# A linear-attention and MLP block on one core: one tile's transpose moved to TensorE, the first block's reciprocals moved to DMA, and the written orders laid out anew

## The chip, the cores and the metric

The kernel runs on one core of a Trainium2 chip. The metric is the device time of one execution in microseconds; the times below are medians of several runs. A profile of one execution goes with them, with every instruction's start and length on each engine: TensorE (PE, its weight loads as PEld), VectorE (DVE), ScalarE (ACT), GpSimd (POOL), and the DMA queue that SyncE (SP) issues.

## The reference

x has 2048 rows of 512 values in bf16. The kernel computes a linear attention with 32 heads of 16 columns and then a two-layer ReLU network of inner width 1792, each on normalized rows and each added to what came in.

```python
qkv = layernorm(x) @ wqkv                     # q, k, v: 32 heads of 16
phi = lambda t: where(t > 0, t + 1, exp(t)) + 1e-6
pq, pk = phi(q), phi(k)
kv  = einsum("bhsd,bhse->bhde", pk, v)
z   = einsum("bhsd->bhd", pk)
num = einsum("bhqd,bhde->bhqe", pq, kv)
den = einsum("bhqd,bhd->bhq", pq, z)[..., None] + 1e-6
h   = x + (num / den) @ wo
h2  = h + relu(layernorm(h) @ w1) @ w2
```

## The kernel before

The 2048 rows lie in 16 tiles of 128 rows (index t) and in four chunks, called blocks here too, of four tiles (index c). The whole program is one list of words, `ORDER`, written out by hand or by a planner; each word is the name of an `op_` function with its indices, and each engine executes its own instructions strictly in the order in which the words stand. Semaphores between the engines are put in from the data that the words read and write. So a word that waits holds up every later word on its engine. All DMAs are issued by SP, in the order of their words.

The words that matter here, with the engine that executes them:

- `lx.t.n` (SP, line 201) loads n tiles of x from tile t on; `lk`, `lq`, `lv`, `lo`, `l1`, `l2` load parts of the weights (line 204).
- `S.t`, `A.t` (VectorE, lines 222 and 223) take mean and variance of tile t; `R.t.n` (ScalarE, lines 228 and 229) the reciprocal deviation by a logarithm and an exponential; `N.t` (VectorE, line 247) writes the normalized tile. Lower-case `s`, `a`, `r`, `n` do the same after the attention.
- A normalized tile has to be transposed into `lnT`, 128 columns by 128 rows four times. Either TensorE does it (`T.t.b`, line 266, into PSUM bank b) and ScalarE copies it out (`E.t`, line 276), or one DMA does it (`X.t`, line 287; `x.t` after the attention, line 288). Before, tiles 0 to 3 go by TensorE and the others by DMA.
- `K.t.b` and `Q.c.j.b` (TensorE, lines 295 and 303) are the projections, four matmuls of 512 columns each. phi takes `F` (exponential, ScalarE, line 313), `U` (ReLU, ScalarE, line 316), `M` (minimum, VectorE, line 320) and `D` (sum, VectorE, line 323); `W` (VectorE, line 328) does the work of U and D in one instruction that reads PSUM. With a q in front (`qF` ...) they work on Q.
- `G.t` (TensorE, line 347) sums the normalized rows times phi(K) over the tiles, in PSUM banks 4 to 7; `za`, `zf`, `z`, `zc`, `zh` sum phi(K) alone. `gD` (VectorE) or `gA` (ScalarE) copies G out, `kv` multiplies it by the weights of v, `kx` masks the heads, `m` multiplies by wo and `mA` copies that out.
- The denominators: `dn.c` (TensorE, line 444) for the four tiles of a chunk, `dnl` (ScalarE, line 450) the logarithm, `dnx.c.t.n` (ScalarE, line 457) the exponential of its negative for n tiles, spread over the columns. The reciprocals are then transposed into `rd`: by a DMA (`dt.t`, line 476), or by TensorE and ScalarE (`rt.t.b`, line 266, and `re.t`, line 468). `dm.c.j.2` (VectorE, line 480) multiplies phi(Q) by them, and `h.t.b` (TensorE, line 490) multiplies by m; `hD` (VectorE, line 496) adds x.
- The network: `p.c.f.b` (TensorE, line 506), `pA` or `pD` (ReLU by ScalarE, line 512, or VectorE, line 517), `f` (TensorE, line 526), `fo` (VectorE, line 534), `fd` (SP, line 541) writes out.

TensorE starts with `warm` matmuls on zeros while the first tiles come in. The tile buffer `rd` holds the reciprocals of one chunk, so each chunk's `dt` waits for the `dm` of the chunk before.

Of the kernel before, what the change touches and what calls it, by code (L numbers as in the profile page):

```python
# [38 lines left out]
p.0.11.1 p.0.8.2 p.0.10.0 dt.14 dt.13 dt.15 f.3.7.0.7 pA.0.10.2 pA.0.8.2 n.5 dt.12 n.6 dm.3.0.2 dm.3.2.2 n.4
s.11 n.7 hD.8 h.14.1 h.13.3 f.0.4.7.7 h.12.0 h.15.6 hD.14 s.10 s.8 s.14 hD.12 s.9 x.5 x.7 x.6 x.4 f.1.5.7.7  # L40
f.3.7.7.7 fo.0 hD.15 p.1.9.1 p.1.8.0 f.2.6.0.7 pA.1.8.2 f.2.6.7.7 p.1.0.0 p.1.1.1 fo.1 a.14 a.10 a.8 fo.3 s.12
a.11 a.12 s.15 a.15 n.11 hD.13 s.13 a.13 a.9 n.8 n.10 p.1.3.3 n.9 n.12 pA.1.0.2 fo.2 x.10 fd.3 x.9 x.8 x.11
p.1.10.6 p.1.4.0 p.1.7.5 fd.0 p.1.5.1 p.1.2.2 p.1.11.7 p.1.6.4 n.14 pD.1.6.2 r.12.4 pA.1.4.2 n.15 n.13
pD.1.10.2 pA.1.2.2 p.2.4.0 p.2.5.1 pA.2.4.2 x.15 f.5.5.0.7 p.2.0.0 p.2.1.1 p.2.2.2 p.2.3.3 pA.2.0.2 p.1.13.1
f.7.7.0.7 p.1.12.0 f.4.4.0.7 pD.2.2.2 pD.1.12.2 p.2.7.3 p.2.6.2 p.2.13.1 f.6.6.0.7 f.7.7.7.7 f.5.5.7.7
p.2.12.0 r.4.4 pD.2.6.2 p.2.10.2 f.6.6.7.7 pA.2.12.2 x.12 x.14 x.13 fd.1 fd.2 p.2.9.1 p.2.11.3 p.2.8.0 fo.7
pA.2.10.2 pD.2.8.2 f.4.4.7.7 p.3.3.3 p.3.9.1 p.3.8.0 fo.4 pA.3.8.2 fo.5 fo.6 f.8.4.0.7 p.3.5.1 p.3.4.0 p.3.2.2
f.9.5.0.7 pD.3.4.2 pD.3.2.2 fd.5 fd.4 p.3.0.0 f.10.6.0.7 f.9.5.7.7 f.10.6.7.7 p.3.6.2 p.3.7.3 p.3.1.1 fd.6
f.8.4.7.7 pD.3.6.2 pA.3.0.2 r.8.4 fo.9 fo.10 p.3.13.1 f.11.7.0.7 p.3.11.3 p.3.12.0 pA.3.12.2 fo.8 f.11.7.7.7
fd.7 fd.9 p.3.10.2 f.12.4.0.7 f.14.6.0.7 fo.11 pD.3.10.2 f.15.5.0.14.3.1 f.12.4.7.7 f.14.6.7.7 fd.8 fd.10  # L50
fd.11 fo.15.3.1 fo.12 fo.14 f.13.5.0.7 f.13.5.7.7 fo.13 f.15.7.0.14.0.2 fd.12 fd.14 fd.13 fd.15.3.1
f.15.4.0.14.2.1 fo.15.0.2 fd.15.0.2 fo.15.2.1 fd.15.2.1
"""


# [521 lines left out]
```

## Time and profile before

| what | value |
|---|---|
| median of 3 runs | 169.99 us (169.94 to 171.55) |
| profiled execution: own time, span | 171.34 us, 169.6 us |
| TensorE busy (share of the span) | 162.6 us (96%) |
| VectorE, ScalarE, GpSimd busy | 102.6, 65.2, 4.9 us |
| granted TensorE clock | 1.00 |
| DMA transposes into lnT before and after the attention, and into rd | 12, 16 and 15 |

The span runs from the first to the last instruction of the profiled execution; its own time, as the runs are timed, is 1.74 us more. Busy times are sums of an engine's records; matmuls are pipelined, so that a record of a 512-column matmul (380 ns on average) is longer than the distance between the starts of two of them (0.216 us). Times of start are microseconds from the span's start. A bracket behind a line of the timeline gives the engine's idle time ahead of it and what ended it.

### The profile page before, as it was taken

The numbers are of one execution on the slowest core, as the hardware profiler recorded it, in microseconds if no ns is written. First come the engines' busy times: TensorE is split into PE (matmuls) and PEld (weight loads), VectorE is DVE, ScalarE is ACT, GpSimd is POOL, SyncE is SP. The second block draws the span as 40 slices with busy tenths as digits, with TensorE's granted clock in tenths as the row PEclk, the third lists the DMA queues.
The fourth block names the chain that finished last, engine by engine and source line by source line (L and its number), as shares of the span: only waits on it lengthen the run. The fifth ranks groups of instructions, "written<-read, shape, count | busy, mean of one in ns | idle before, by whom it ended". The sixth has DMA issues, their size and how long they took to land.

```text
span 169.6 us, 2272 instructions
## 1 busy us (share of the span) xinstructions
PE 162.6 (96%) x847; PEld 75.6 (45%) x863; DVE 102.6 (61%) x203; ACT 65.2 (38%) x98; POOL 4.9 (3%) x21
## 2 busy tenths in 40 slices
...
GB/s 128 312 192 142 110 81 125 270 395 261 65 122 203 108 64 66 62 31 95 60 69 0 9 115 62 69 120 1 0 0 0 124 0 4 0 93 31 0 66 62
DMA packets 31675, 15.75 MB, mean 93 GB/s; under 512 B 24240, under 2 KB 30640, under 8 KB 31664
## 3 DMA queue, kind: packets, MB, share of 16 engines
...
q8 instruction: 7, 0.11, 0.3%
...
HBM read 7.86 MB, written 2.10 MB: 59 GB/s over the span
## 4 chain that ended last, share of the span: by engine, by line
PE 83%; DMA 7%; DVE 5%; SPq 2%; issue 2%; ACT 0%; DVEq 0%
PE bk L526 28%; PE bk L506 28%; PE bk L490 9%; PE bk L303 6%; PE bk L347 6%; PE bk L295 4%; DMA x_nat<-in_A_x_dram 3%; DMA lnT<-h_nat 2%; DVE st L222 2%; DMA rd<-wk_sb 2%; SPq L201 1%; DVE h_nat L247 1%; DVE eb L320 1%; PE bk L444 1%; PE bk L388 1%
## 5 line engine op out<-in xcount | busy, mean ns | idle before, releaser
L526 PE MATMUL bk<-w_sb,at 128*128 128x512 bf16 (+2 forms) x248 | 51.2, 355 | 0.2
L506 PE MATMUL bk<-lnT,w_sb 128*128 128x512 bf16 x220 | 50.9, 380 | 0.2
L512 ACT ACTIVATE at<-bk 128x1024 bf16<-128x1024 f32 x17 | 17.2, 1022 | 67.3 <-PE bk L506 60.9
L526 PEld LDWEIGHTS <-at 128*128 128x128 bf16 x252 | 23.5, 98 | 25.2
L506 PEld LDWEIGHTS <-w_sb 128*128 128x128 bf16 x224 | 21.7, 98 | 26.0
L517 DVE TENSOR_SCALAR at<-bk 128x1024 bf16<-128x1024 f32 x11 | 13.4, 1223 | 32.7 <-PE bk L506 32.6
L534 DVE SCALAR_TENSOR_TENSOR gT<-bk,rstd,h_nat 128x512 bf16<-128x512 f32 (+2 forms) x18 | 12.0, 688 | 15.9 <-PE bk L526 14.8
L313 ACT ACTIVATE eb<-bk 128x1024 bf16<-128x1024 f32 (+1 forms) x18 | 16.4, 924 | 4.0 <-PE bk L295 2.4
L295 PE MATMUL bk<-wk_sb,lnT 128*128 128x512 bf16 x63 | 15.3, 380 | 0.7 <-DMA lnT<-h_nat 0.5
L490 PE MATMUL bk<-m_sb,pqs 128*128 128x512 bf16 x61 | 15.1, 380 | 0.2
L303 PE MATMUL bk<-lnT,wq_sb 128*128 128x512 bf16 x61 | 14.6, 379 | 0.1
L496 DVE TENSOR_TENSOR h_nat<-bk,x_nat 128x512 bf16<-128x512 f32 x16 | 10.8, 684 | 4.7 <-PE bk L490 4.7
L316 ACT ACTIVATE rb<-bk 128x1024 bf16<-128x1024 f32 (+1 forms) x14 | 12.5, 901 | 2.6 <-PE bk L303 1.9
L347 PE MATMUL bk<-at,h_nat 128*128 128x512 bf16 x56 | 13.4, 379 | 0.1
L222 DVE BATCH_NORM_STATS2 st<-x_nat 128x6 f32<-128x512 bf16 x16 | 10.7, 677 | 3.1 <-DMA x_nat<-in_A_x_dram 3.1
L224 DVE BATCH_NORM_STATS2 st<-h_nat 128x6 f32<-128x512 bf16 x16 | 10.7, 682 | 0.1
L347 PEld LDWEIGHTS <-h_nat 128*128 128x128 bf16 x64 | 6.2, 98 | 8.7 <-issue 1.5
L490 PEld LDWEIGHTS <-pqs 128*128 128x128 bf16 x64 | 5.9, 98 | 8.7 <-DVE pqs L480 2.0
L295 PEld LDWEIGHTS <-lnT 128*128 128x128 bf16 x64 | 6.0, 98 | 8.3 <-DMA lnT<-h_nat 1.4
L303 PEld LDWEIGHTS <-wq_sb 128*128 128x128 bf16 x64 | 6.1, 97 | 6.9
L457 ACT ACTIVATE wk_sb<-ld 128x1024 bf16<-128x1024 f32 (+1 forms) x9 | 8.2, 951 | 0.1
L480 DVE TENSOR_TENSOR pqs<-pqT,rd 128x1024 bf16<-128x1024 bf16 x8 | 5.2, 685 | 4.4 <-DMA rd<-wk_sb 2.6
...
## 6 DMA issues: line engine op xcount, KB each, us to landing
...
```

What stands on the lines that cost most here:

```text
L222: op_S = lambda t: nc.vector.bn_stats(out=st[:, t, :], in_=x_nat[:, t, :])
L295: nc.tensor.matmul(bk[:, b, :], lhsT=lnT[c][:, kd, j * P : (j + 1) * P], rhs=wk_sb[:, kd, :], start=(kd == 0), stop=(kd == KD - 1),)
L303: nc.tensor.matmul(bk[:, b, :], lhsT=wq_sb[:, kd, j * P : (j + 1) * P], rhs=lnT[c][:, kd, :], start=(kd == 0), stop=(kd == KD - 1),)
L313: nc.scalar.activation(out=buf(eb, kind, i, n), in_=bank(at_bank[kind, i], n), func=ACT.Exp)
L316: nc.scalar.activation(out=buf(rb, kind, i, n), in_=bank(at_bank[kind, i], n), func=ACT.Relu)
L347: nc.tensor.matmul(bk[:, KD + kd, :], lhsT=ln_nat[:, t, kd * P : (kd + 1) * P], rhs=pk(t)[:, 0, :], start=(t == 0), stop=(t == NT - 1),)
L490: nc.tensor.matmul(bk[:, b, :], lhsT=pqs[:, (c * KD + jb) % NQ, j * P : (j + 1) * P], rhs=m_sb[:, jb, :], start=(jb == 0), stop=(jb == KD ...
L506: nc.tensor.matmul(bk[:, b, cols], lhsT=w1_sb[:, kd, f * P : (f + 1) * P], rhs=lnT[c][:, kd, cols], start=(kd == 0), stop=(kd == KD - 1),)
L512: nc.scalar.activation(out=acts[c % 2][:, f : f + n, :], in_=bank(at_bank["p", c, f], n), func=ACT.Relu)
L517: nc.vector.tensor_scalar(out=acts[c % 2][:, f : f + n, :], in0=bank(at_bank["p", c, f], n), scalar1=0.0, scalar2=None, op0=ALU.max,)
L526: nc.tensor.matmul(bk[:, b, 0 : w * P], lhsT=acts[c % 2][:, f, j * P : (j + 1) * P], rhs=w2_sb[:, f, k * P : (k + w) * P], start=(f == 0), ...
L534: nc.vector.scalar_tensor_tensor(out=o_t[:, t % NO, cols], in0=bk[:, at_bank["f", t, k], 0 : w * P], scalar=rstd2[:, t : t + 1], in1=h_nat ...
```

## The change

Nothing is computed in another way, and no function that runs is altered (`op_warmq` is added and not called). The list `ORDER` is written anew:

- `X.5` (a DMA) is replaced by `T.5.0` and `E.5` (TensorE and ScalarE). The transposes T.2, T.1 and T.3 go to banks 0, 7 and 6, K.0 and K.1 to banks 4 and 7.
- `rt.3.3` and `re.3` (TensorE and ScalarE) are replaced by `dt.3` (a DMA), and the two exponentials `dnx.0.3.1` and `dnx.0.2.1` by one, `dnx.0.2.2`.
- `W` on VectorE and `U` with `D` are exchanged in four places: `W.14`, `qW.0.2` and `qW.3.2` become U and D, `qU.1.0` with `qD.1.0` becomes `qW.1.0`. `gD.2.2` becomes `gA.2.2` (ScalarE). The ReLUs of p are divided anew: eleven by VectorE and seventeen by ScalarE before, thirteen and fifteen after.
- On SP the order of the loads of x stays; `lq.0.2` moves behind the transposes X.4 to X.10, `lv.2.2` ahead of X.15 and X.14, `l2.0.7` ahead of the first `dt` and `l1.0.2` behind `dt.3`.
- On VectorE `S` of a later tile stands earlier against `N` and `D` (S.5 ahead of N.3, S.7 ahead of S.6 and M.0, A.6 and A.7 ahead of D.0), on ScalarE `R` stands earlier (R.4 ahead of F.0, R.6 ahead of U.1). `dn.0` goes ahead of `G.15`.

The first half of the list, before and after (the rest, from the attention's output of the second chunk on, is the same work with `h`, `p` and `f` in another sequence and other banks):

```diff
-const table lx.0.1 lx.2.1 S.0 lx.1.1 S.2 A.0 S.1 A.2 R.0.1 N.0 R.2.1 lx.3.1 lk.0.2 lx.4.2 warm.1.7 warm.9.7
-A.1 R.1.1 T.0.6 S.3 N.2 N.1 A.3 E.0 lk.2.2 warm.1.7 R.3.1 S.4 T.2.7 lx.6.2 E.2 N.3 S.5 T.1.4 A.4 K.0.1 E.1 A.5
-F.0.1 R.4.2 S.6 T.3.2 K.1.0 M.0.1 E.3 U.0.1 lx.8.4 K.2.3 F.1.1 N.5 masks U.1.1 N.4 S.7 D.0.1 M.1.1 A.7 A.6
-R.6.2 D.1.1 K.3.2 F.2.1 F.3.1 U.2.1 U.3.1 S.9 N.6 lx.12.4 X.5 G.0 X.4 G.1 M.2.1 A.9 S.8 N.7 A.8 M.3.1 D.2.1
-R.8.2 K.5.1 lq.0.2 D.3.1 N.9 K.4.0 F.4.2 X.6 S.13 N.8 X.7 G.2 A.13 S.12 M.4.2 X.9 A.12 G.3 U.4.2 R.12.2 K.6.2
-X.8 D.4.2 K.7.3 N.12 S.10 S.11 N.13 G.4 K.9.1 K.8.0 F.6.2 U.6.2 A.11 M.6.2 A.10 X.12 R.10.2 D.6.2 X.13 N.11
-S.15 N.10 A.15 za.2 U.8.2 F.8.2 S.14 M.8.2 A.14 G.5 G.6 G.7 X.11 K.12.0 X.10 K.13.1 K.11.3 R.14.2 lq.2.2 za.4
-N.14 D.8.2 K.10.2 N.15 za.6 X.14 F.12.2 U.12.2 X.15 F.10.2 G.8 Q.0.0.0 Q.0.1.1 M.12.2 lv.2.2 l1.0.2 l1.2.2
-lo.0.4 lv.0.2 U.10.2 K.14.2 G.9 K.15.3 D.12.2 M.10.2 za.8 D.10.2 qU.0.0.2 G.10 za.10 qF.0.0.2 F.14.2 qM.0.0.2
-za.12 Q.0.2.0 Q.0.3.1 G.11 M.14.2 zf.12 qF.0.2.2 G.12 W.14.2 qM.0.2.2 l2.7.7 qD.0.0.2 G.13 z.1.2.14 z.3.2.14
-z.2.2.14 z.0.2.14 zc qW.0.2.2 G.14 G.15 zh dn.0.0 dnl.0 dnx.0.0.2 gD.2.2 gD.0.2 Q.1.0.2 Q.1.1.3 Q.1.3.1 kv.2.4
-kv.3.4 dnx.0.3.1 dnx.0.2.1 kv.1.4 kv.0.4 Q.1.2.0 kx qF.1.0.2 qU.1.0.2 m.0.4 rt.3.3 m.2.6 m.1.5 Q.2.0.2 m.3.7
-dt.1 qM.1.0.2 qF.1.2.2 dt.0 dt.2 re.3 qD.1.0.2 Q.2.1.3 mA.0.2 qM.1.2.2 l2.0.7 mA.2.2 qW.1.2.2 dn.1.5 dm.0.0.2
-Q.2.3.1 dnl.1 dnx.1.0.2 dm.0.2.2 h.3.5 hD.3 dnx.1.2.2 qF.2.0.2 qU.2.0.2 s.3 h.1.4 hD.1 a.3 s.1 h.0.5 Q.2.2.0
-n.3 hD.0 dt.5 dt.6 h.2.4 qU.2.2.2 qF.2.2.2 a.1 s.0 dt.7 hD.2 n.1 s.2 a.0 n.0 dt.4 dm.1.0.2 Q.3.0.2 Q.3.1.3
-Q.3.3.1 Q.3.2.0 dm.1.2.2 a.2 x.3 h.4.6 h.7.4 qU.3.0.2 qF.3.0.2 x.1 h.6.5 h.5.7 qF.3.2.2 n.2 qM.2.2.2 qM.2.0.2
-qD.2.0.2 qM.3.0.2 qD.2.2.2 x.0 dn.2.3 x.2 dnl.2 dnx.2.2.2 p.0.0.2 p.0.1.3 hD.4 qM.3.2.2 qW.3.2.2 qD.3.0.2
-pD.0.0.2 hD.7 hD.5 dnx.2.0.2 p.0.3.1 dn.3.6 p.0.2.0 dt.10 dt.11 hD.6 s.5 s.4 dt.8 dt.9 p.0.5.3 p.0.4.2
...
+const table lx.0.1 lx.2.1 S.0 lx.1.1 S.2 A.0 S.1 A.2 R.0.1 masks N.0 R.2.1 lx.3.1 lk.0.2 lx.4.2 warm.1.7
+warm.9.7 A.1 R.1.1 T.0.6 S.3 N.2 N.1 A.3 E.0 S.4 R.3.1 lk.2.2 S.5 warm.1.7 T.2.0 N.3 T.1.7 E.2 lx.6.2 A.4 E.1
+K.0.4 K.1.7 A.5 R.4.2 lx.8.4 S.7 S.6 F.0.1 M.0.1 N.5 A.6 U.0.1 A.7 T.3.6 D.0.1 E.3 lx.12.4 N.4 F.1.1 R.6.2
+K.2.3 U.1.1 K.3.2 S.8 T.5.0 X.4 M.1.1 A.8 N.7 S.9 D.1.1 E.5 X.7 G.0 K.5.1 N.6 A.9 F.3.1 F.2.1 S.13 R.8.2 U.2.1
+M.2.1 N.9 U.3.1 S.10 D.2.1 S.12 M.3.1 A.10 G.1 K.4.0 U.4.2 A.13 N.8 A.12 F.4.2 X.6 R.12.2 X.9 K.7.3 S.11 M.4.2
+D.3.1 N.12 A.11 G.2 K.6.2 X.8 D.4.2 N.13 S.14 K.9.1 X.12 F.6.2 U.6.2 R.10.2 G.3 G.4 K.8.0 G.5 X.13 M.6.2 N.10
+A.14 N.11 D.6.2 F.8.2 U.8.2 za.2 S.15 M.8.2 A.15 X.11 G.6 G.7 R.14.2 K.12.0 X.10 D.8.2 N.15 N.14 za.4 K.13.1
+K.11.3 K.10.2 za.6 lq.2.2 lq.0.2 za.8 U.12.2 F.12.2 F.10.2 U.10.2 G.8 lv.2.2 M.10.2 M.12.2 D.10.2 X.15 X.14
+D.12.2 za.10 G.9 Q.0.1.1 Q.0.0.0 qF.0.0.2 qU.0.0.2 K.15.3 K.14.2 G.10 Q.0.2.0 Q.0.3.1 l1.2.2 lo.0.4 F.14.2
+U.14.2 qM.0.0.2 za.12 qF.0.2.2 qU.0.2.2 G.11 zf.12 M.14.2 G.12 D.14.2 qM.0.2.2 z.1.2.14 G.13 z.0.2.14 z.2.2.14
+qD.0.0.2 l2.0.7 lv.0.2 z.3.2.14 l2.7.7 qD.0.2.2 zc zh G.14 dn.0.0 G.15 dnl.0 dnx.0.0.2 gA.2.2 Q.1.1.3 Q.1.0.2
+gD.0.2 dnx.0.2.2 kv.1.4 kv.3.4 kv.0.4 kv.2.4 Q.1.2.0 Q.1.3.1 qF.1.0.2 dt.1 kx qM.1.0.2 qW.1.0.2 m.2.6 m.0.4
+m.1.5 qF.1.2.2 qM.1.2.2 Q.2.0.2 m.3.7 Q.2.1.3 dt.0 mA.0.2 qW.1.2.2 dt.2 dt.3 mA.2.2 dn.1.5 l1.0.2 Q.2.3.1
+dnl.1 dm.0.0.2 dnx.1.0.2 dm.0.2.2 h.3.4 hD.3 h.1.5 s.3 hD.1 h.0.4 Q.2.2.0 h.2.5 hD.0 s.1 a.3 s.0 dnx.1.2.2 n.3
+qU.2.0.2 qF.2.0.2 qF.2.2.2 qU.2.2.2 dt.4 dt.6 dt.5 dt.7 Q.3.0.2 Q.3.1.3 a.1 hD.2 a.0 n.1 n.0 s.2 qF.3.0.2 x.3
+dm.1.0.2 Q.3.3.1 Q.3.2.0 x.0 qU.3.0.2 qU.3.2.2 qF.3.2.2 dm.1.2.2 h.4.6 h.5.4 x.1 h.6.7 a.2 h.7.1 n.2 qM.2.0.2
+qM.3.0.2 qM.2.2.2 qD.2.2.2 qD.2.0.2 dn.2.3 dnl.2 hD.4 x.2 dnx.2.2.2 r.0.4 dnx.2.0.2 p.0.0.2 p.0.1.3 qD.3.0.2
+hD.7 qM.3.2.2 hD.6 pD.0.0.2 qD.3.2.2 p.0.3.1 p.0.2.0 p.0.5.3 p.0.4.2 pD.0.2.2 s.6 hD.5 pA.0.4.2 dn.3.6 p.0.7.1
...
```

More of the change, by code (lines that the diff above doesn't have):

```diff
@@ L34 @@
-Q.3.3.1 Q.3.2.0 dm.1.2.2 a.2 x.3 h.4.6 h.7.4 qU.3.0.2 qF.3.0.2 x.1 h.6.5 h.5.7 qF.3.2.2 n.2 qM.2.2.2 qM.2.0.2
-qD.2.0.2 qM.3.0.2 qD.2.2.2 x.0 dn.2.3 x.2 dnl.2 dnx.2.2.2 p.0.0.2 p.0.1.3 hD.4 qM.3.2.2 qW.3.2.2 qD.3.0.2
-pD.0.0.2 hD.7 hD.5 dnx.2.0.2 p.0.3.1 dn.3.6 p.0.2.0 dt.10 dt.11 hD.6 s.5 s.4 dt.8 dt.9 p.0.5.3 p.0.4.2
-dm.2.2.2 s.7 a.7 dm.2.0.2 r.0.4 pA.0.2.2 dnl.3 pA.0.4.2 p.0.7.1 p.0.6.0 dnx.3.2.2 pA.0.6.2 p.0.13.3 f.0.4.0.7
-p.0.12.2 pA.0.12.2 f.1.5.0.7 h.9.3 h.10.1 h.11.0 h.8.6 dnx.3.0.2 a.4 s.6 hD.9 a.5 a.6 hD.10 hD.11 p.0.9.3
@@ L39 @@
[L39 to L52, printed above, removed]
+const table lx.0.1 lx.2.1 S.0 lx.1.1 S.2 A.0 S.1 A.2 R.0.1 masks N.0 R.2.1 lx.3.1 lk.0.2 lx.4.2 warm.1.7
+warm.9.7 A.1 R.1.1 T.0.6 S.3 N.2 N.1 A.3 E.0 S.4 R.3.1 lk.2.2 S.5 warm.1.7 T.2.0 N.3 T.1.7 E.2 lx.6.2 A.4 E.1
@@ new lines @@
+hD.7 qM.3.2.2 hD.6 pD.0.0.2 qD.3.2.2 p.0.3.1 p.0.2.0 p.0.5.3 p.0.4.2 pD.0.2.2 s.6 hD.5 pA.0.4.2 dn.3.6 p.0.7.1
+p.0.6.0 dt.10 dt.9 dt.8 dt.11 s.5 dm.2.2.2 dm.2.0.2 pA.0.6.2 p.0.12.2 p.0.13.3 dnl.3 dnx.3.0.2 dnx.3.2.2 s.7
+pA.0.12.2 f.3.7.0.7 h.11.6 h.8.5 h.10.4 p.0.9.3 p.0.11.1 hD.11 s.4 p.0.10.0 hD.10 hD.8 h.9.6 p.0.8.2 f.1.5.0.7
+dt.15 dt.13 s.8 dt.14 dt.12 dm.3.0.2 a.4 a.6 a.5 a.8 dm.3.2.2 pA.0.8.2 pA.0.10.2 n.4 s.11 a.7 n.7 hD.9
+f.0.4.0.7 f.3.7.7.7 f.1.5.7.7 h.15.1 h.13.2 h.14.3 h.12.6 s.10 n.5 n.6 s.9 fo.1 a.11 a.9 hD.15 hD.12 f.0.4.7.7
```

15 lines of the change are left out of this document (added).

## Prediction

> **What bounds the kernel now.** I read the page first (busy shares, groups), then the chain that ended last in order of time, then the waits, then the windows, and last the timelines of the engines around the places where TensorE waits.
>
> ```profile
> span 169.6 us, 2272 instructions
> PE 162.6 (96%) x847; PEld 75.6 (45%) x863; DVE 102.6 (61%) x203; ACT 65.2 (38%) x98; POOL 4.9 (3%) x21
> ...
> PE bk L347 <- DVE pk_lo L323: 1.2, 1, 1.2
> PE bk L295 <- DMA lnT<-h_nat: 0.5, 1, 0.5
> ...
> 5.50:12.39 6.89, 5.26 (x35) 1.00 0.74 245
> 12.39:21.75 9.36, 8.79 (x39) 1.00 0.60 127
> 21.75:50.41 28.66, 28.36 (x185) 1.00 0.66 186
> 50.41:62.80 12.39, 12.34 (x68) 1.00 0.59 143
> 62.80:166.90 104.10, 103.56 (x514) 1.00 0.20 45
> ```
>
> TensorE is busy for 96% of the span, so only its gaps can be won. The five window rows (stretch, its length, TensorE busy) place them: 1.6 us before 12.39, 0.6 up to 21.75, 0.3 up to 50.41, and after that almost nothing (0.05, and 0.5 that lies in single skips of one matmul's length, which I take for missing records). Whatever the new orders do, the sum has to come from the first 50 us. The chain and the timelines there show what each gap waits for:
>
> ```profile
> 4.12 5.74 DMA x_nat<-in_A_x_dram
> ...
> 18.33 3.38 DMA lnT<-h_nat
> ...
> 46.53 3.04 DMA rd<-wk_sb
> ...
> 49.66 0.70 DVE pqs L480
> 50.36 0.05 issue
> 50.41 3.08 PE bk L490 x12
> ```
>
> The load of tiles 6 and 7 of x, issued at 4.12, lands 5.74 later. The transpose of tile 8 lands at 21.71. The last transpose of the first block's reciprocals lands at 49.57, then VectorE multiplies (`dm`), and the first `h` starts at 50.41. These are the three places that the change touches.
>
> **The first 21.75 us.** The first two rows are groups of the page by shape (count | busy, mean ns) that are used further down; the others are the timeline around the late load, whose start times also give how long one instruction holds its engine:
>
> ```profile
> L517 DVE TENSOR_SCALAR at<-bk 128x1024 bf16<-128x1024 f32 x11 | 13.4, 1223 | 32.7 <-PE bk L506 32.6
> ...
> L328 DVE SCALAR_TENSOR_TENSOR pqT<-bk,eb 128x1024 bf16<-128x1024 f32 x3 | 3.7, 1222 | 0.1
> ...
> 7.33 1.06 ACT L276 ACTIVATE lnT<-bk 128x512 bf16<-128x512 bf16 x2
> ...
> 8.39 0.30 DVE L223 BATCH_NORM_AGGREGATE mv<-st 128x2 f32<-128x6 f32 x2
> ...
> 8.45 2.77 PE L295 MATMUL bk<-wk_sb,lnT 128*128 128x512 bf16 x12
> 8.76 0.30 ACT L228 ACTIVATE rstd<-mv,eps 128x2 f32<-128x2 f32 x1
> ...
> 9.88 0.69 DVE L222 BATCH_NORM_STATS2 st<-x_nat 128x6 f32<-128x512 bf16 x1 [1.19 <-DMA x_nat<-in_A_x_dram]
> ...
> 10.49 0.28 DVE L320 TENSOR_SCALAR eb<-eb 128x512 bf16<-128x512 bf16 x1
> ...
> 10.68 0.73 DVE L247 TENSOR_SCALAR h_nat<-x_nat,mv,rstd 128x512 bf16<-128x512 bf16 x2
> ...
> 11.32 0.69 DVE L222 BATCH_NORM_STATS2 st<-x_nat 128x6 f32<-128x512 bf16 x1
> 11.93 0.41 DVE L323 TENSOR_TENSOR pk_lo<-rb,eb 128x512 bf16<-128x512 bf16 x1
> ...
> 12.39 1.89 PE L347 MATMUL bk<-pk_lo,h_nat 128*128 128x512 bf16 x7 [1.17 <-DVE pk_lo L323]
> ...
> 12.45 0.24 DVE L223 BATCH_NORM_AGGREGATE mv<-st 128x2 f32<-128x6 f32 x2
> ...
> 21.75 1.04 PE L295 MATMUL bk<-wk_sb,lnT 128*128 128x512 bf16 x4 [0.52 <-DMA lnT<-h_nat]
> ```
>
> A statistics instruction (`S`) holds VectorE 0.61 us, `M` 0.20, `N` 0.32 (two take 0.73, one 0.41), `D` 0.32, `A` 0.09; a small copy or exponential on ScalarE holds it 0.48, the pair `R` 0.45. `D.0` begins at 11.93 and `G.0` at 12.39, 0.46 later. Four matmuls of 512 columns take 0.86 (twelve of them run from 8.45 to 11.06), four transposes 0.22.
>
> The loads of x are issued in the same order as before, so tiles 6 and 7 land at 9.85 again. In the new order VectorE then runs S.7, S.6, M.0, N.5, A.6, A.7, D.0: 9.88 + 0.61 + 0.61 + 0.20 + 0.32 + 0.09 + 0.09 = 11.80 for D.0, and **G.0 at 12.26 instead of 12.39**. One statistics instruction still stands ahead of D.0 twice over, so the wait doesn't go; it is split. On TensorE: K.1 ends at 9.31 (it starts at 8.45, behind E.1, as before), T.3 to 9.53, K.2 to 10.39. K.3 needs E.3, which stands on ScalarE behind R.4, F.0 and U.0: R.4 at 8.6 (behind the two A, 8.39 and 8.48, where it began at 8.76 before), F.0 9.03, U.0 9.51, E.3 9.99, so K.3 at 10.63, ends 11.49. T.5 needs N.5 (11.30 + 0.41 + 0.05 = 11.76) and ends at 11.98: this is tile 5's transpose, 0.22 us of TensorE and one 0.58 copy (E.5) in place of a DMA. It lies in the gap ahead of G.0 and costs nothing; without that gap it would cost 0.22. G.0 ends at 13.12. K.5 needs E.5, and there the new order adds a wait: R.6 stands ahead of U.1 and E.5 on ScalarE and waits for A.7 at 11.89; then U.1 12.34, E.5 12.82, K.5 at 13.46 (a gap of 0.34), to 14.32. D.1 waits for that U.1 and stands behind N.4, S.8, M.1, A.8, N.7, S.9: 14.24, so G.1 at 14.70 (a gap of 0.38), to 15.56. Then K.4, K.7, G.2, K.6, K.9, G.3 without a wait (six by 0.864, 20.75), G.4 at about 20.85 behind D.4, and **K.8 at 21.71**. Its transpose, X.8, can be issued at 18.45 behind N.8 and takes 2.5 to 3.4, landing at 20.9 to 21.9. Before, K.8 began at 21.75, after the same tiles. Many small waits replace two large ones: a gain of 0.04, bounds -0.3 to +0.2.
>
> **From K.8 to the first h.** The wq and wv loads now go ahead of X.15 and X.14 on SP's queue. Three loads of 256 KB, issued from about 25.4 where one alone lands 2.9 after its issue, land by about 30, ahead of Q.0.1 at 30.3; X.15 lands by about 31 for K.15 at 32.0, X.14 a microsecond later for K.14 at 32.9. That cover is about a microsecond; if it goes, K.15 waits for what is over. TensorE's work up to h.3 is the same less the four transposes `rt` (0.22) that the reciprocals lose, plus about 0.15 because Q.2.0's bank is now emptied by VectorE's `qW` (1.22 long) where ScalarE did it. 21.71 + 28.36 - 0.22 + 0.15 = **50.0: TensorE reaches h.3 there**. What it needs by then is all four reciprocal tiles:
>
> ```profile
> 42.14 2.09 ACT L457 ACTIVATE wk_sb<-ld 128x1024 bf16<-128x1024 f32 x3
> 43.22 4.53 SPq L476 DMA_TRANSPOSE rd<-wk_sb  x3
> 47.02 0.59 ACT L468 ACTIVATE rd<-bk 128x512 bf16<-128x512 bf16 x1
> ...
> L476 SPq DMA_TRANSPOSE rd<-wk_sb x15: 1189/1202/1983, 43.2 to 78.0; - x15
> ...
> DMA to landing us min/median/max: 2.4/2.4/4.0
> ```
>
> Before, `dt.1`, `dt.0`, `dt.2` go by DMA from 43.22 (the first exponential's end) to 49.57, 6.35 us, and tile 3 by TensorE and ScalarE, finished at 47.61 and hidden. Undisturbed, three would take two issues of 1.25 and a landing of 2.45, 4.95 us; here the first one took 4.0 to land and one issue 1.98. Now dn.0 stands ahead of G.15 (0.86 earlier) and K.8 is 0.04 earlier, so the first exponential ends and dt.1 is issued 0.9 earlier, at 42.3, and dt.3 goes fourth, 1.25 more:
>
> - undisturbed, all land at 42.3 + 3 x 1.25 + 2.45 = 48.5, and h.3 starts when TensorE gets there, 50.0: 0.4 earlier, and 0.16 more because the second half of the products is no longer late. Sum -0.57.
> - disturbed as before, they land at 42.3 + 6.35 + 1.25 = 49.9; 0.08 + 0.75 (from 49.57 over `dm` at 49.66 to 50.41) give h.3 at **50.74: +0.33**.
>
> I take the second: it is the same three transposes from the same queue, at the same place in the program, with the last big weight load landing just ahead (landed at 42.05, row below). The exponential of tiles 2 and 3 is now behind the copy gA on ScalarE (1.0), ends at 44.1, and dt.2 isn't issued before 44.8, so that costs nothing.
>
> ```profile
> L204 SPq DMA_DIRECT2D w_sb<-in_B_w_dram x1: 485/485/485, 32.4 to 32.4; - x1
> ...
> DMA to landing us min/median/max: 9.7/9.7/9.7
> ```
>
> The Trainium skill, page "VectorE: DVE Perf Modes", section "The three transpose paths", gives 390 ns for a 128x128 transpose on TensorE and 1309 ns by DMA, and advises TensorE wherever PSUM will do as destination; by it this half of the change goes the wrong way. As an estimate from that page four blocks would be 5.2 us by DMA, which would put dt.3 at 52.3 and h.3 2.7 us later; the rows show 2.4 for the four blocks, and the measurement decides.
>
> **After h.3** the same chain follows as before: VectorE (hD, s, a, n of four tiles, then dm.1) is the same list, and from there TensorE has no gaps that could be won. New tight places are those where VectorE empties banks in ScalarE's stead: pD.1.0 (1.22) must be done within a run of 1.5 us on TensorE, and I find it done about 0.1 ahead. Bounds 0 to +0.4; I take 0, because this cover is there in every place that I went through. The last eight words are the same work in nearly the same order, so the tail stays.
>
> **The sum.** The K.8 term of -0.04 is swallowed by the wait for the reciprocals, so +0.33 on the span: 169.6 to 169.9; the execution's own time goes from 171.34 (its span and 1.74 around it) to 171.7. The median of the runs is 169.99, 1.35 below that execution; the same difference gives **170.3**.
>
> **Rivals.**
> 1. *Undisturbed transposes* (the first bullet): 169.99 - 0.57 = 169.4. For it: all but a few of the 15 take 2.4. Against it: the disturbed ones are at this very place. Chance 0.22.
> 2. *Slower: the reciprocals by DMA come later still.* It decides as soon as they land after 49.6, and from there each microsecond is one of the span, since nothing stands ahead of h.3 that TensorE could do. The price comes from a second disturbance, where one transpose took 4.9 to land and the one issued behind it 4.0, 1.55 over the usual 2.45:
>
> ```profile
> L288 SPq DMA_TRANSPOSE lnT<-hn x1: 1267/1267/1267, 84.2 to 84.2; - x1
> ...
> DMA to landing us min/median/max: 4.9/4.9/4.9
> ...
> DMA to landing us min/median/max: 4.0/4.0/4.0
> ```
>
>    On top of the first disturbance, 49.9 + 1.55 + 0.83 = 52.3, +1.9: 171.9. Against it: two such in four transposes are seen nowhere. The rule of the Trainium skill above points this way too. Chance 0.15.
> 3. *Faster: the change does what it says*, and both waits on x (1.2 and 0.5) and the reciprocals' wait go: -1.2 - 0.5 - 0.4 = -2.1, 167.9. For it: 0.22 us of T.5 lies in the gap. Against it: D.0 still stands behind two statistics of the late tiles. Chance 0.06.
> 4. *The timed runs get x earlier than the profiled one*, which would explain its 1.35. Then the 1.19 us that VectorE waits at 9.88 go before and after, but the new order keeps its small waits on ScalarE (K.3 0.24, K.5, G.1): about +0.5, 170.5. Chance 0.07.
>
> The forecast's own case has 0.50. **How the numbers follow:** a measurement of this kernel tells about 1% (1.7 us) from no change. Only rival 2 is slower by more, only rival 3 faster by more: faster 0.06, same 0.79, slower 0.15. The range reaches from rival 1 with its head bound (169.4 - 0.3) to nearly rival 2: 169.1 to 171.8.
>
> **What would show it.** Right: G.0 near 12.3, gaps of 0.2 to 0.4 at K.3, K.5 and G.1, K.8 near 21.7, dt.1 issued near 42.3 and dt.3 landing near 49.9, h.3 near 50.7, and no TensorE gap above 0.2 after 60. It would be wrong if Q.0 or K.15 waits for wq or for X.15, if the transposes land before 49.0 or after 51, or if a gap shows behind pD in the second half.

## The result and the profile after

| | before | after |
|---|---|---|
| median of 22 runs each, on one chip | 170.35 us (169.94 to 171.55) | 171.28 us (170.25 to 172.30) |
| ratio | | 1.0042 [1.0026, 1.0059] |
| profiled execution: own time, span | 171.34, 169.6 us | 170.98, 169.3 us |

By the ratio the kernel is slower by 0.42%, 0.72 us (the medians lie 0.93 apart): within the 1% that the prediction called no change, but not zero. The ratios here and below leave out a few executions that fell into a slower state; the medians of the experiments hold them. The profiled execution of after is shorter than that of before by 0.3 us, against the medians. So the two profiles can't simply be subtracted; each stage has to be compared by itself. First the page of after:

```profile
span 169.3 us, 2262 instructions
PE 162.3 (96%) x847; PEld 75.8 (45%) x863; DVE 102.7 (61%) x204; ACT 65.6 (39%) x98; POOL 4.8 (3%) x21
...
q8 instruction: 7, 0.11, 0.3%
```

Then its windows (stretch, its length, TensorE busy), cut at the same words as before: first G, K.8, first h, first p.

```profile
11.65:20.68 9.03, 8.85 (x43) 3.77 (x41) 9.03 (x29) 7.96 (x16) 0.00 (x0) 1.00 0.45 89
20.68:49.13 28.45, 28.03 (x180) 13.80 (x185) 23.87 (x40) 19.72 (x24) 0.00 (x0) 1.00 0.77 198
49.13:61.55 12.42, 12.13 (x68) 5.35 (x68) 11.55 (x26) 9.45 (x11) 0.00 (x0) 1.00 0.59 151
61.55:165.90 104.35, 103.75 (x514) 48.95 (x524) 49.10 (x85) 20.81 (x29) 0.00 (x0) 1.00 0.20 44
```

TensorE is as full as before: 1.5 us in which it isn't busy in these four stretches, and 1.5 in the same four before. The chain that ended last shows what each of the first three places waits for now:

```profile
4.12 0.47 SPq L201
4.63 6.58 DMA x_nat<-in_A_x_dram
...
17.15 3.49 DMA lnT<-h_nat
20.69 1.04 PE bk L299 x4
...
48.49 0.81 PE bk L307 x3
49.29 1.05 PE bk L494 x4
...
59.09 2.42 DMA lnT<-hn
61.55 5.35 PE bk L510 x24
```

In this execution tiles 6 and 7 of x landed at 8.57 (4.46 after their issue; before 9.85, 5.74), and the load that the chain goes through is the next one, of tiles 8 to 11. K.8 waits for its transpose as before, which took 3.49. The first `h` follows TensorE's own work without a step between. The first `p` waits for `x.2` to 61.51, a wait that the chain of before doesn't have: there the first `p` (62.80) follows `dn.2` on TensorE.

The end is where the two profiles differ against the new order. The timeline of after around the last `f` words:

```profile
160.77 5.06 PE L530 MATMUL bk<-w_sb,at 128*128 128x512 bf16 x39
...
162.05 2.26 DVE L538 SCALAR_TENSOR_TENSOR gT<-bk,rstd,h_nat 128x512 bf16<-128x512 f32 x3 [5.64 <-PE bk L530]
163.49 3.84 SPq L545 DMA_DIRECT2D out_dram<-gT  x6
165.09 0.48 DVE L538 SCALAR_TENSOR_TENSOR gT<-bk,rstd,h_nat 128x256 bf16<-128x256 f32 x1 [0.78 <-PE bk L530]
165.88 0.35 DVE L538 SCALAR_TENSOR_TENSOR gT<-bk,rstd,h_nat 128x128 bf16<-128x128 f32 x1 [0.30 <-PE bk L530]
```

Its stores (`fd`, L545; ns that one holds SP's queue, min/median/max, and first and last start) in two windows, first the two issued at 163.49 and 163.87, then the one at 164.34:

```profile
L545 SPq DMA_DIRECT2D out_dram<-gT x2: 333/382/431, 163.5 to 163.9; - x2
...
DMA to landing us min/median/max: 3.1/3.1/3.2
...
L545 SPq DMA_DIRECT2D out_dram<-gT x1: 1532/1532/1532, 164.3 to 164.3; - x1
```

And the DMA queues (packets, MB, share of 16 engines) over the 1.08 us behind 164.53:

```profile
q8 instruction: 1, 0.02, 6.3%
```

Before, the timeline of the same place:

```profile
164.65 0.75 DVE L534 SCALAR_TENSOR_TENSOR gT<-bk,rstd,h_nat 128x512 bf16<-128x512 f32 x1 [2.27 <-PE bk L526]
166.18 0.48 DVE L534 SCALAR_TENSOR_TENSOR gT<-bk,rstd,h_nat 128x256 bf16<-128x256 f32 x1 [0.78 <-PE bk L526]
166.96 0.35 DVE L534 SCALAR_TENSOR_TENSOR gT<-bk,rstd,h_nat 128x128 bf16<-128x128 f32 x1 [0.30 <-PE bk L526]
```

and the store that is issued last, at 167.34:

```profile
L541 SPq DMA_DIRECT2D out_dram<-gT x1: 332/332/332, 167.3 to 167.3; - x1
...
DMA to landing us min/median/max: 1.4/1.4/1.4
```

Before, the three full-width `fo` of the last chunk stand 1.5 and 3 us apart (160.12, 161.63, 164.65); after, they run back to back from 162.05, so the six stores come in one bunch. At 164.53 a load of instructions (the queue "q8 instruction", one packet of 16 KB) runs through the same DMA engines for 1.08 us. Two stores then take 3.1 to 3.2 us to land, and the issue of the next one holds SP's queue for 1.53 us. The last `fo` ends at 166.23 (165.88 + 0.35), but its store isn't issued before 166.92, 0.69 late; before, it was issued 0.03 after. From the start of the last `f` (f.15.4) to the end of the span it is 3.75 us before and 4.49 after; this stretch is called the tail.

The rest of this document reads all profiles by the starts of the same five words on TensorE. The times are read from the weight loads of each trace:

| kernel | K.8 | first h, after K.8 | first p, after first h | f.15.4, after first p | end, after f.15.4 |
|---|---|---|---|---|---|
| before | 21.75 | 28.66 | 12.26 | 103.20 | 3.75 |
| before_newtail | 20.60 | 28.70 | 12.29 | 103.20 | 5.25 |
| before_shift | 21.21 | 28.49 | 12.63 | 103.21 | 3.75 |
| before_dt | 22.16 | 28.61 | 12.35 | 103.21 | 3.87 |
| after | 20.68 | 28.43 | 12.44 | 103.23 | 4.49 |
| after_again | 21.11 | 28.89 | 12.26 | 103.24 | 3.76 |
| after_oldtail | 20.74 | 29.43 | 12.26 | 103.23 | 3.95 |
| after_rt | 20.57 | 28.47 | 12.25 | 103.60 | 4.41 |
| after_rt_shift | 20.68 | 28.45 | 12.64 | 103.25 | 3.81 |
| after_x5 | 21.82 | 29.05 | 12.28 | 103.23 | 3.86 |
| after_shift | 20.98 | 29.14 | 12.35 | 103.25 | 3.75 |
| after_oldhead | 20.68 | 28.48 | 12.45 | 103.23 | 3.98 |
| after_shift_early | 22.00 | 28.24 | 12.63 | 103.23 | 3.75 |

### The profile page after: what moved, and what is told of

Read it like the earlier page. It is cut to its first block, busy times and chain, and to the rows that moved or that the text cites. A ratio compares the mean times of both kernels' runs of the same rounds, so it can differ in the third digit from the quotient of the medians.

```text
span 169.3 us, 2262 instructions
## 1 busy us (share of the span) xinstructions
PE 162.3 (96%) x847; PEld 75.8 (45%) x863; DVE 102.7 (61%) x204; ACT 65.6 (39%) x98; POOL 4.8 (3%) x21
## 4 chain that ended last, share of the span: by engine, by line
PE 75%; DVE 9%; DMA 7%; ACT 2%; issue 2%; SPq 2%; DVEq 0%
PE bk L530 29%; PE bk L510 28%; PE bk L351 5%; PE bk L494 5%; DMA x_nat<-in_A_x_dram 4%; PE bk L299 4%; PE bk L307 4%; DMA lnT<-h_nat 2%; DVE st L226 2%; SPq L201 2%; DVE h_nat L500 2%; DMA lnT<-hn 1%; DVE eb L324 1%; DVE st L228 1%; ACT wk_sb L461 1%
## 5 line engine op out<-in xcount | busy, mean ns | idle before, releaser
L510 PE MATMUL bk<-lnT,w_sb 128*128 128x512 bf16 x218 | 50.2, 379 | 0.5 <-DMA lnT<-hn 0.2
L516 ACT ACTIVATE at<-bk 128x1024 bf16<-128x1024 f32 x15 | 14.9, 1022 | 70.5 <-PE bk L510 50.6
L521 DVE TENSOR_SCALAR at<-bk 128x1024 bf16<-128x1024 f32 x13 | 15.9, 1221 | 26.9 <-PE bk L510 16.8
L320 ACT ACTIVATE rb<-bk 128x1024 bf16<-128x1024 f32 (+1 forms) x16 | 14.4, 913 | 1.4 <-PE bk L299 1.4
L461 ACT ACTIVATE wk_sb<-ld 128x1024 bf16<-128x1024 f32 x8 | 8.2, 1049 | 0.1
L484 DVE TENSOR_TENSOR pqs<-pqT,rd 128x1024 bf16<-128x1024 bf16 x8 | 5.2, 685 | 3.5 <-DMA rd<-wk_sb 3.5
```

Of the source, the lines that this page charges most:

```text
L320: nc.scalar.activation(out=buf(rb, kind, i, n), in_=bank(at_bank[kind, i], n), func=ACT.Relu)
L510: nc.tensor.matmul(bk[:, b, cols], lhsT=w1_sb[:, kd, f * P : (f + 1) * P], rhs=lnT[c][:, kd, cols], start=(kd == 0), stop=(kd == KD - 1),)
L516: nc.scalar.activation(out=acts[c % 2][:, f : f + n, :], in_=bank(at_bank["p", c, f], n), func=ACT.Relu)
L521: nc.vector.tensor_scalar(out=acts[c % 2][:, f : f + n, :], in0=bank(at_bank["p", c, f], n), scalar1=0.0, scalar2=None, op0=ALU.max,)
```

## The experiments

The expectations name their theories. TAIL: the new order of the last `f`, `fo` and `fd` costs the time. RECIPROCALS: the fourth transpose by DMA (`dt.3`) makes the first `h` wait, as predicted. HEAD: the new order up to G.8 costs it. BOTH: the tail and the reciprocals, each a part. Ratios are to the kernel before, run on the same chip in the same set.

**after_oldtail: the last words in before's sequence.**

```diff
-f.14.6.0.7 f.15.5.0.14.3.1 f.12.4.0.7 fd.11 fo.15.3.1 f.13.5.0.7 f.12.4.7.7 f.14.6.7.7 f.13.5.7.7 fo.14 fo.12
-fo.13 f.15.7.0.14.0.2 fo.15.0.2 f.15.4.0.14.2.1 fo.15.2.1 fd.12 fd.14 fd.15.3.1 fd.13 fd.15.0.2 fd.15.2.1
+f.12.4.0.7 f.14.6.0.7 fd.11 f.15.5.0.14.3.1 f.12.4.7.7 f.14.6.7.7 fo.15.3.1 fo.12 fo.14 f.13.5.0.7 f.13.5.7.7
+fo.13 f.15.7.0.14.0.2 fd.12 fd.14 fd.13 fd.15.3.1 f.15.4.0.14.2.1 fo.15.0.2 fd.15.0.2 fo.15.2.1 fd.15.2.1
```

> The changed kernel with the last 22 words in the order of before (f.12 ahead of f.14, fo.12 ahead of fo.14, fd.13 ahead of fd.15.3.1). Theory TAIL: in the changed kernel fd.12, fd.14 and fd.15.3.1 are issued within 0.9 us of each other just when TensorE's last load of instructions goes through a DMA engine, the issue of fd.15.3.1 takes 1.5 us, and the last two stores go out 0.7 us late in every run. Then this kernel is about 0.7 us faster than the changed one, 0 to 0.2 us slower than before, the last store is issued within 0.05 us of the end of fo.15.2.1, and from the end of the last matmul to the end of the span it is 3.0 us instead of 3.7. Theory RECIPROCALS (the fourth DMA transpose costs the time) and theory HEAD (the small waits of the first 21 us cost it): the same time as the changed kernel, 0.4 to 0.5% slower than before.

Measured: 170.95 us, ratio 1.0018 [0.9999, 1.0036]. In the profile the stores around an instruction load at 165.20 look like this (the two issued at 165.22 and 165.60, then the last):

```profile
L545 SPq DMA_DIRECT2D out_dram<-gT x2: 332/722/1112, 165.2 to 165.6; - x2
...
DMA to landing us min/median/max: 2.2/2.3/2.3
...
L545 SPq DMA_DIRECT2D out_dram<-gT x1: 381/381/381, 167.3 to 167.3; - x1
```

An issue is stretched here too (1.11 us), but the last `fo` ends at 167.10 and its store leaves at 167.28, so that only 0.18 is lost: the tail is 3.95. The spread-out order takes the load almost without loss. The ratio is lower than after's by 0.24%; the intervals overlap.

**before_newtail: before, with nothing but after's last words.** The same edit the other way round.

> The kernel before with the last 26 words in the order of the changed kernel, nothing else. TAIL: 0.6 to 0.8 us slower than before (ratio about 1.004), with the stretched issue of fd.15.3.1 in the profile. RECIPROCALS and HEAD: the same as before within 0.1 us.

Measured: 171.78 us, ratio 1.0047 [1.0021, 1.0073]. The last words alone bring as much as the whole change. In its profile the load comes a little later, at 166.90, and hits the very last store. Five of the stores first, then the last one, issued at 166.25:

```profile
L544 SPq DMA_DIRECT2D out_dram<-gT x5: 332/398/439, 163.5 to 165.6; - x5
...
DMA to landing us min/median/max: 1.5/1.8/1.9
...
L544 SPq DMA_DIRECT2D out_dram<-gT x1: 333/333/333, 166.3 to 166.3; - x1
...
DMA to landing us min/median/max: 3.0/3.0/3.0
```

The DMA queues from 166.90 to 168.20:

```profile
q8 instruction: 1, 0.02, 6.0%
```

The last store, of that size, lands in 1.4 to 1.5 otherwise; here it took 3.0, and the tail is 1.5 longer than in before.

**after_rt: tile 3's reciprocals by TensorE and ScalarE again.**

```diff
-gD.0.2 dnx.0.2.2 kv.1.4 ... Q.1.2.0 Q.1.3.1 qF.1.0.2 dt.1 ... dt.2 dt.3 mA.2.2
+gD.0.2 dnx.0.3.1 dnx.0.2.1 kv.1.4 ... Q.1.2.0 rt.3.7 Q.1.3.1 qF.1.0.2 re.3 dt.1 ... dt.2 mA.2.2
```

> The changed kernel with the reciprocals of tile 3 by TensorE and ScalarE again (rt.3 into bank 7 behind Q.1.2, re.3 behind qF.1.0, two exponentials in place of one), so three DMA transposes for the first block. RECIPROCALS: the row of DMA transposes dt, dt, x that ends with x.2 starts 0.6 us earlier, p.0.0 starts 0.3 to 0.5 us earlier, and the kernel is 0.3 to 0.5 us faster than the changed one. TAIL and HEAD: within 0.2 us of the changed kernel (the four transposes cost TensorE 0.22).

Measured: 171.04 us, ratio 1.0017 [0.9992, 1.0043]; the tail of its profile is hit (4.41). Nothing is settled by the ratio alone. By the table the first `h` comes 28.47 and 28.45 after K.8 in the two kernels of the new order with `rt.3`, and 28.24 to 29.43, on average 28.81, in the seven with `dt.3`. In after_rt 0.37 more than in the other kernels lies between the first `p` and the last `f`; what it is stays open.

**after_x5: tile 5 by DMA again in the new order.**

```diff
-S.8 T.5.0 X.4 M.1.1 A.8 N.7 S.9 D.1.1 E.5 X.7
+S.8 X.5 X.4 M.1.1 A.8 N.7 S.9 D.1.1 X.7
```

> The changed kernel with tile 5 transposed by a DMA again (X.5 ahead of X.4 in SP's queue, T.5 and E.5 left out). HEAD: if T.5 with E.5 in ScalarE's row costs time, this is 0.2 to 0.4 us faster than the changed kernel, with K.5 at once behind G.0. TAIL and RECIPROCALS: the same as the changed kernel within 0.2 us; X.5 is one more DMA ahead of X.4, X.7, X.6, so K.4 could wait for up to 0.5 us.

Measured: 171.50 us, ratio 1.0024 [0.9999, 1.005]. On TensorE K.5 now waits for that transpose:

```profile
12.16 1.07 PE L350 MATMUL bk<-pk_lo,h_nat 128*128 128x512 bf16 x4
14.24 1.04 PE L298 MATMUL bk<-wk_sb,lnT 128*128 128x512 bf16 x3 [1.01 <-DMA lnT<-h_nat]
```

Taking out this named part of the change makes a new wait of a microsecond in this order, so the run can't tell whether `T.5` costs anything. The kernel has 859 pairs of weight load and matmul in place of 863, its profile shows no instruction load in the tail, and the tail is 3.86.

**after_again: after once more,** on the chip of the next three.

> The changed kernel once more, as the reference of this group on its chip, and for a second profile. All theories: 0.3 to 0.6% slower than before. TAIL: from the start of the last f to the end of the span 4.4 to 5.2 us, with a store whose issue is stretched or which lands over 2.5 us after its issue; the kernel before had 3.75.

Measured: 171.55 us, ratio 1.0022 [0.9992, 1.0052]. In this profile the tail is undisturbed, 3.76: the stores from 164.2 on (first rows) land in their usual times. The seventh instruction load starts at 170.93, behind the span's end (last row, DMA queues from 170.9 to 172.4).

```profile
L545 SPq DMA_DIRECT2D out_dram<-gT x6: 332/363/449, 164.2 to 167.0; - x6
...
DMA to landing us min/median/max: 1.4/1.7/1.9
...
q8 instruction: 1, 0.02, 5.7%
```

Yet the execution is a long one: its own time is 171.99 us, 2.7 more than its span of 169.3. In all 93 executions of before that ran beside the experiments this difference is 1.66 to 1.89. It is 2.0 to 3.1 in 4 of 22 executions of after, 5 of 12 of after_again, 4 of 12 of after_oldhead and 3 of 12 of after_x5, and in none of the other kernels. The spans of after_again are on average no longer than those of before on its chip (169.25 and 169.32): on average its loss lies behind the last instruction and not among the stores. That the late load makes it is likely, since the kernels with long executions are those in whose profiles the seventh load comes behind the span or isn't seen, and after itself, the same program as after_again; it isn't shown, for in the profile of after_oldhead the load is late too (169.22) and the difference is 1.7.

**after_shift and before_shift: 14 small matmuls more.** They go ahead of the first `p`, on zeros into a bank that nobody reads, 64 columns each. Their work is small beside what they do to the count of pairs: the seven loads of 16 KB come 112 to 137 pairs apart in the profile of after, 125 on average, and 14 more pairs are to pull the last one out of the tail.

```diff
-dnx.2.0.2 p.0.0.2
+dnx.2.0.2 warms.14.2 p.0.0.2
```

> The changed kernel with 14 small matmuls (64 columns, into a bank that the next word overwrites) ahead of p.0.0, where TensorE waits for x.2. They compute nothing that is used. They move every later load of TensorE's instructions 14 matmuls earlier, the last one from 164.5 to about 161.5 us, ahead of the last stores. Theory TAIL (the stores collide with that load): no store is stretched, from the start of the last f to the end of the span 3.75 us or less, and the kernel is 0.5 to 0.8 us faster than the changed one, less 0.1 to 0.2 for the small matmuls. Theory ORDER (the loss comes from the order of the stores alone, whatever is loaded): no gain, 0.2 us slower than the changed one.

> The kernel before with the same 14 small matmuls ahead of p.0.0. TAIL: the load at 165.3 us moves to about 162; it cost the kernel before little in its profile (a store issue of 0.80, landings of 1.9), so 0.2 us slower to 0.3 us faster than before. ORDER: 0.2 us slower.

Measured: after_shift 170.73 us, ratio 0.9987 [0.996, 1.0013]; before_shift 171.08 us, ratio 1.0012 [0.998, 1.0043]. The DMA queues of after_shift from 162.0 to 163.2, where the load of 162.18 lies:

```profile
q8 instruction: 1, 0.02, 4.6%
```

and its stores:

```profile
L545 SPq DMA_DIRECT2D out_dram<-gT x6: 332/366/449, 164.4 to 167.2; - x6
...
DMA to landing us min/median/max: 1.4/1.7/1.9
```

The load now runs ahead of the first store; the same bunched stores land within 1.9 us and the tail is 3.75. Against after_again on the same chip the edit gains 0.35%, although it adds work (the two intervals overlap); in before, whose tail had little to lose, it gains nothing. So the order of the stores alone costs nothing in this profile, and a load alone cost before little. But the gain isn't only the tail's: of the 0.57 us between the means of the two, 0.37 lie behind the span.

**after_oldhead: before's words up to G.8, then after's** (with four small matmuls at the start, which keep the count of pairs at 863).

```diff
-K.0.4 K.1.7 A.5 R.4.2 lx.8.4 S.7 S.6 F.0.1 ... T.5.0 X.4 ... E.5 X.7 G.0 K.5.1 ... G.8
+K.0.1 E.1 A.5 F.0.1 R.4.2 S.6 T.3.2 K.1.0 ... X.5 G.0 X.4 G.1 ... K.5.1 lq.0.2 ... G.8
```

> The first part of the kernel before, up to G.8 (tile 5 by DMA, the loads of wq in their old places, the old order of S, N, D and R), then the rest of the changed kernel; four small matmuls at the start keep the count of TensorE's instructions, so that the last load of instructions falls where it does in the changed kernel. Theory HEAD (the new first part costs time against the old one): 0.3 to 0.6 us faster than the changed kernel, K.8 to G.8 earlier for like landings of x. TAIL: within 0.2 us of the changed kernel on average; slower by up to 0.3 when x lands late, since the old part waits for it at G.0 and K.8.

Measured: 171.55 us, ratio 1.0035 [1.0009, 1.0061]. With the old head the loss stays, so HEAD falls. Its profile, its fastest execution, shows an undisturbed tail (3.98), so that where the others lose is not seen; 4 of the 12 end late, as said above. The profile reaches K.8 at 20.68, exactly where after's does: with x early, both heads end at the landing of X.8 at 20.64.

**after_rt_shift: after_rt and after_shift together.**

> The changed kernel with two edits: the reciprocals of tile 3 by TensorE and ScalarE again, and the 14 small matmuls ahead of p.0.0 that move the last load of TensorE's instructions ahead of the last stores. Theory BOTH (the tail and the fourth DMA transpose each cost the changed kernel 0.3 to 0.4 us on average): h.3 starts without a wait, p.0.0 waits at most 0.3 us for x.2, no store is stretched, 0.2 to 0.5 us faster than the kernel with the small matmuls alone, 0.3 to 0.5% faster than before. Theory TAIL alone: the same as with the small matmuls alone, about 0.1% faster than before.

Measured: 170.91 us, ratio 1.0014 [0.9989, 1.004]. A gain over before was expected under BOTH and didn't come, nor did the 0.1% expected under TAIL, which lies at the edge of the interval. Against after_rt (1.0017, on another chip) the shift gains nothing here that can be told, which doesn't bear TAIL out. Its profile has one of the two shortest spans, 168.8 us, with nothing lost at the first `h` or in the tail, but the median of its runs isn't below before's. So the part of the reciprocals in the time isn't shown.

**after_shift_early: the shift made at the start,** in the place of two of the nine `warm`.

```diff
-warm.9.7 A.1
+warm.7.7 warms.14.7 A.1
```

> The changed kernel with two of the nine large warm-up matmuls replaced by 14 small ones, which take as long: all loads of TensorE's instructions come 12 matmuls earlier, from 22.3, 43.0, 63 and 164.5 us to about 19.5, 40.5, 60.5 and 162. Theory LOADS (a transpose that is in flight when instructions are loaded lands 0.6 to 1.5 us late): the load at 40.5 is over before dt.1 is issued at 41.3, dt.1 lands in 2.5 us in place of 3.95, dt.3 lands at 47.5 in place of 48.3 for like landings of x, and h.3 doesn't wait; the load at 60.5 meets x.2 or x.1 and p.0.0 waits 0.5 us or more longer; the tail is undisturbed; in sum 0 to 0.5 us faster than the changed kernel. If dt.1 still takes 4 us, LOADS falls.

Measured: 172.15 us, ratio 1.0082 [1.005, 1.0115], a miss: it is slower, though the last load is out of the tail (163.17, tail 3.75). The table puts the loss ahead of K.8 (22.00, 1.32 later than after). Two things add up there. K.0 waits for the second weight load, tiles 6 and 7 of x land at 9.56 in place of 8.57, and X.8, tile 8's transpose, is issued 0.84 later than in after (17.99, 17.15):

```profile
8.44 0.81 PE L299 MATMUL bk<-wk_sb,lnT 128*128 128x512 bf16 x3 [0.64 <-DMA wk_sb<-in_A_wqkv_dram]
```

Why loads that were issued at the same times should land later when TensorE runs other matmuls beside them isn't settled; one profile can't tell it from the scatter of these loads. The other 0.48 belongs to the moved loads. X.8, for which K.8 waits, took 3.97 to land in place of 3.49 (first rows), and two instruction loads ran while it was under way, at 19.86 and 19.91 (DMA queues from 19.8 to 20.9):

```profile
L291 SPq DMA_TRANSPOSE lnT<-h_nat x1: 1188/1188/1188, 18.0 to 18.0; - x1
...
DMA to landing us min/median/max: 4.0/4.0/4.0
...
q8 instruction: 1, 0.02, 5.2%
q14 instruction: 1, 0.01, 1.8%
```

Of LOADS the other part came true: the load that met dt.1 in after came ahead of it here (41.59), dt.1 took 2.4 in place of 3.95, and the first `h` follows K.8 sooner than in any other kernel (28.24).

**before_dt: before, with the reciprocals alone changed** (`dt.3` for `rt.3` and `re.3`, one exponential for two, four small matmuls for the count of pairs).

```diff
-warm.9.7 A.1 ... kv.3.4 dnx.0.3.1 dnx.0.2.1 kv.1.4 ... m.0.4 rt.3.3 m.2.6 ... dt.2 re.3 qD.1.0.2
+warm.9.7 warms.4.7 A.1 ... kv.3.4 dnx.0.2.2 kv.1.4 ... m.0.4 m.2.6 ... dt.2 dt.3 qD.1.0.2
```

> The kernel before with the reciprocals alone changed: rt.3, re.3 and the split exponential out, one exponential for tiles 2 and 3, dt.3 as the fourth DMA behind dt.2 (four small matmuls at the start keep the count of TensorE's instructions). Theory RECIPROCALS: dt.3 lands 0.5 to 1.3 us after the third transpose did, h.3 waits that much longer, and the kernel is 0.4 to 1.0 us (0.25 to 0.6%) slower than before. TAIL alone: the same as before within 0.2 us.

Measured: 170.97 us, ratio 1.001 [0.9981, 1.0038]: no loss that can be told. The last two of the four transposes:

```profile
L479 SPq DMA_TRANSPOSE rd<-wk_sb x2: 1211/1238/1264, 46.2 to 47.5; - x2
...
DMA to landing us min/median/max: 2.5/2.8/3.2
```

and VectorE's wait for them on the timeline:

```profile
50.02 1.29 DVE L483 TENSOR_TENSOR pqs<-pqT,rd 128x1024 bf16<-128x1024 bf16 x2 [0.70 <-DMA rd<-wk_sb]
```

`dt.3` is issued at 47.48 and lands at 49.94, 6.31 after the first one's issue, as long as the three took before (6.35). The first `h` comes 28.61 after K.8, against 28.66. Here the fourth transpose cost nothing, but the first two ran undisturbed (2.41 and 2.47 from issue to landing): the instruction load that met dt.1 in before (45.07) came ahead of it here (42.91). So the edit took the disturbance away as well, and what `dt.3` costs by itself isn't told.

**What the set says together.** With the new last words and a load that can fall among them (after, after_again, after_rt, after_oldhead, before_newtail) the ratios are 1.0042, 1.0022, 1.0017, 1.0035 and 1.0047, 1.0033 on average. With before's last words or the load moved away (after_oldtail, after_shift, before_shift, after_rt_shift, before_dt) they are 1.0018, 0.9987, 1.0012, 1.0014 and 1.0010, 1.0008 on average. (after_x5 and after_shift_early, with other losses ahead of K.8, are in neither.) The difference, 0.25% or 0.4 us, is an estimate of what the last words cost on average, with a load that hits the stores, comes late or misses both. About 0.14 of it lies behind the span, by the means of own time less span. The two groups were made after the results: with after_x5 and after_shift_early in the second one its average would be 1.0021 and the difference 0.12%. The clearest single run is before_newtail, whose interval lies above 1 with nothing but the last words changed. No version here beats the kernel before by more than the measurement can tell; after_shift comes nearest.

## Why the prediction was right, and where it was not

The range, 169.1 to 171.8, held the time, and no change within 1% was the likeliest case. The forecast of 170.3 is 0.98 too low. Of this 0.36 is its base: the median of the three runs shown was 169.99, that of 22 runs 170.35. The rest, 0.6, is in the main a term that the sum had at nothing. That the time came out near the forecast is in part luck: in the profiles the term of +0.33 came out at -0.23 and the one of 0 at +0.74.

1. **The step that failed: "The last eight words are the same work in nearly the same order, so the tail stays".** The work is the same, but the order puts three `fo` back to back and the stores in a bunch where the last instruction load falls. The term was 0 and measured 0.74 in the profile (4.49 against 3.75), 1.5 in before_newtail, and 0.4 on average over the sets, about a third of that behind the span. The page of before showed "q8 instruction"; the prediction never asked where its seven packets lie.
2. **The reciprocals, +0.33.** The mechanism was half right. dt.1 left 20.61 after K.8 (41.29; predicted 20.6) and took 3.95 to land, as disturbed as before, and the issue behind it 1.99, and the third landed 6.48 after the first one's issue (before 6.35). But the third was a disturbed one (3.15) and the fourth was not (2.48), so that it landed 0.57 behind it and not 1.25: at 48.34, 27.66 after K.8, where 28.2 was predicted. The reason that the prediction gave for the disturbance, the last big weight load just ahead, doesn't fit: in the profile of before no DMA packet moved from 42.8 to 44.2. An instruction load ran while dt.1 was under way, at 45.07 before and at 43.14 after. In ten of the thirteen profiles one did, and dt.1 took 3.7 to 4.4; in before_dt and after_shift_early the load came ahead of it, and it took 2.4. VectorE's wait for `dt.3` (`dm`, L484) in the timeline of after:

```profile
48.37 1.29 DVE L484 TENSOR_TENSOR pqs<-pqT,rd 128x1024 bf16<-128x1024 bf16 x2 [0.52 <-DMA rd<-wk_sb]
```

   and TensorE's first `h`, which follows the last matmul of Q without a wait:

```profile
48.49 0.81 PE L307 MATMUL bk<-lnT,wq_sb 128*128 128x512 bf16 x3
49.13 1.63 PE L494 MATMUL bk<-m_sb,pqs 128*128 128x512 bf16 x6
```

   In other executions of the new order the first `h` waited up to a microsecond. By the table's averages (28.81 with `dt.3`, 28.46 with `rt.3`) the term is about 0.3, as large as forecast, but the timed runs don't confirm it. The Trainium skill's page "VectorE: DVE Perf Modes", section "The three transpose paths", was the source of an estimate of 5.2 us for the four blocks of a tile. That estimate isn't borne out: dt.3 landed 2.48 after its issue, and rival 2, for which the prediction took that page's rule as speaking, didn't come about. (Nor does the 52.3 of that estimate follow from its terms; 49.9 - 2.45 + 5.2 is 52.65.)
3. **The head, -0.04.** Of the small waits the one at K.3 came, on the copy E.3 of ScalarE (its weight load in the timeline of after):

```profile
10.61 0.55 PEld L299 LDWEIGHTS <-lnT 128*128 128x128 bf16 x4 [0.58 <-ACT lnT L280]
```

   K.2's four matmuls begin at 9.44 and take 0.86, so TensorE is free from 10.30 to 10.61, 0.31 where 0.24 was predicted. K.5 and G.1 lost nothing, since x was early and R.6 didn't hold ScalarE. K.8 came at 20.68, not 21.71, but so it did in the two profiles with before's head and x early (20.60, 20.68). With either head the chain runs from a load of x over VectorE to X.8, and X.8 was slow in all three (3.40 to 3.49), with an instruction load under way (q14, 19.01 in after; 20.16 in before, where it took 3.38); transposes without one took 2.46 (median over the thirteen profiles). So the wait at K.8, 0.52 of TensorE's time in before, goes with a load as the loss in the tail does; the prediction took 2.5 to 3.4 for X.8 without asking what makes the difference. That the order of the head is neutral was right in these profiles.
4. **Rival 4's premise was right:** the profile of before was one with a late x, and others get it earlier. Its price of 0.5, from small waits on ScalarE, didn't show.
5. **After h.3, 0.** Right for the whole network: 103.20 before, 103.23 after, so no `pD` came too late. Missed was the first `p`: it waits for `x.2`, the eighth transpose in a row on SP's queue, and comes 12.44 after the first `h`, where it came 12.26 after it before: 0.18. Four other profiles of the new order have 12.25 to 12.28, so that this is no fixed cost.

Taken from K.8 on, so that the landing of x drops out, the stages of the two profiles sum to -0.23 (K.8 to h) + 0.18 + 0.03 + 0.74 = +0.72 us, and the runs show +0.72 as well. That the two agree so well is luck: the first and the last of these terms scatter by half a microsecond or more from execution to execution, and 0.15 of the runs' 0.72 lies behind the span, where the sum has nothing. What stays open is how the 0.72 divides: the last words have about 0.4 of it by the experiments, and the rest, the reciprocals among it, is below what these runs can tell.
